# Attention ahead of two expert layers: exponentials behind all maxima of their banks, new engine orders, diagonal forms of q copied by GpSimd

## The chip, the core and the metric

The program runs on one core of a Trainium2 chip. Its time is the device time of one execution in microseconds. TensorE (PE) multiplies, VectorE (DVE), ScalarE (ACT) and GpSimd (POOL) work beside it, and SyncE (SP) issues most transfers. Each engine takes its instructions in the order in which the program gives them.

## The reference

Inputs are in float32. First comes attention over 2 batches, 8 heads, 576 rows and 64 columns a head, with a mask by blocks of 64 rows; then two layers of experts on the 1152 rows of 512 columns.

```python
scores = (1 / np.sqrt(D)) * np.matmul(q, k.transpose(0, 1, 3, 2))
scores = np.where(block_i >= block_j, scores, -1e9)
attn = np.exp(scores - np.max(scores, axis=-1, keepdims=True))
attn = attn / (np.sum(attn, axis=-1, keepdims=True) + 1e-09)
x = np.matmul(attn, v)            # heads side by side: rows of 512 columns
# layer 1: the best of 8 experts for each row, relu(x @ w1[e]) @ w2[e], times two gates
# layer 2: the same with one gate, and at most `capacity` rows an expert, in order of the rows
```

## The kernel before, in words

**Precision.** A matmul operand is held as two halves, a high one (`kh`, `nh`, `wh`, `xh`: a copy rounded by ACT) and a low one (`kl`, `nl`, `wl`, `xl`: the rest, by VectorE), and three products replace one.

**Packs and stages.** A head's nine blocks of rows, of both batches, are split into three packs (L96). Pack 0 has four units: block pairs of 384 columns at columns 0 (unit 0) and 512 (unit 1), and of 128 columns at 896 (unit 2) and 384 (unit 3). Pack 1 has two units of 512 columns. Pack 2 has three single blocks: 576 columns at 256 (unit 0), 256 at 0 (unit 1), 192 at 832 (unit 2). A unit's scores lie in a tile `s` of two PSUM banks of 512 columns each, of which there are two. A stage is one pack of one head, 24 in all: heads 0 to 4 one after the other with packs 0, 1, 2 each, and then heads 5, 6, 7 with pack 0 of all three, pack 1 of all three, pack 2 of all three.

**A stage's work.** TensorE makes the scores; VectorE takes the maximum of each unit (`greatest`, tile `mx`, "m0" to "m3"); ACT takes the exponential with that maximum and sums it (`power`, tile `p`, "e0" to "e3"); TensorE turns the results in groups (`transp`, into a bank `pst`); ACT copies the first group out and VectorE the others (`turned`, tile `tp`, "tp0" to "tp2"); TensorE multiplies by v (`pv`, into the one bank `po`); ACT copies that out (`put_out`, tile `ot` or `of`); TensorE multiplies by an identity beside gate columns (`with_gates`, "mv", into the same bank); and VectorE divides by the sums (`inverse`, "ri") and stores rows and gate logits (`results`, "x", tiles `x` and `lg`). GpSimd adds the logits over heads, except for the last head.

**q and k of a head.** TensorE turns them ("K", "Q" for the first 512 rows and "R" for the last 64), ACT makes high halves and VectorE low halves. Pack 2's single blocks need q in diagonal form (`qh`, `ql`: each batch's 64 columns in their own quarter, the rest zero). For blocks 2 and 3 this is "B", read from Q's bank; for block 8 it is part of "R".

**The order.** For stage i the loop of L1803 puts into TensorE's queue: R's turns, the scores of stage i+1, mv of i-2, the turned groups of i, K and Q of a later head, pv of i-1. ACT's and VectorE's queues follow the lists `ORDER` by the pack of stage i; their m and e are those of stage i+1, ri, x and ot those of i-2, tp that of i. `weave` (L1742) then takes, in rounds, the head of each queue whose named predecessors are done, and issues it. That order is the program; the class `InOrder` (L32) keeps it on each engine. Waits between engines follow from it: an instruction waits for earlier accesses of the same tile by another engine. Other instructions, of GpSimd and the routing's small steps, are placed by a planner.

**Into the first expert layer.** When head 7's pack 0 is stored, a routing of the first 384 rows begins (`begin_first`): three products ("route1" to "route3") with small VectorE steps between, the load of the chosen expert's weights, and the gathers of three items' rows by GpSimd. The weights' splits W0 to W3 (`split_hi`, L196) are tied to instructions of the last stage (L1874), the low ones (`split_lo`, L214) to the routing's results. Behind the last mv, `xprep` (L811) turns the first item's rows, and `begin_known` (L982) starts its products and the routing of all rows (L593).

Of the kernel before, what the change touches and what calls it, by code (L numbers as in the profile page):

```python
# [50 lines left out]
def kernel(  # L51
# [1312 lines left out]
    with ExitStack() as actx:  # L1364
# [127 lines left out]
        def q_high(h):  # L1492
            s = st[h]
            for n in ("nh", "nl"):
                s[n] = ap3.tile([P, NC4 * P], F32R, tag=n, name=f"{n}{h}")
            AS.activation(s["nh"], s["ps"]["q"], AF.Copy, scale=SCALE)

        def q_low(h):
            s = st[h]
            AV.scalar_tensor_tensor(out=s["nl"], in0=s["ps"]["q"], scalar=SCALE, in1=s["nh"].bitcast(F32), op0=ALU.mult, op1=ALU.subtract)  # L1500

        def blocks(ps):
            return [ps[r, :].rearrange("p (b j) -> p b j", j=BLK) for r in halves]

        def b_high(h, ps, b0, b1):
            for r, x in zip(halves, blocks(ps)):
                AS.activation(st[h]["qh"][r, b0:b1, r], x, AF.Copy, scale=SCALE)

        def b_low(h, ps, b0, b1):
            for r, x in zip(halves, blocks(ps)):  # L1510
                AV.scalar_tensor_tensor(out=st[h]["ql"][r, b0:b1, r], in0=x, scalar=SCALE, in1=st[h]["qh"][r, b0:b1, r].bitcast(F32), op0=ALU.mult, op1=ALU.subtract)
# [199 lines left out]
        def route_steps(n):  # L1711
            for _ in range(n):
# [15 lines left out]
            ),  # L1728
# [26 lines left out]
        def bank(*names):  # L1755
# [8 lines left out]
            "B": (("S", lambda h: b_high(h, st[h]["ps"]["q"][:, 2 * BLK : 4 * BLK], 0, 2)), ("V", lambda h: b_low(h, st[h]["ps"]["q"][:, 2 * BLK : 4 * BLK], 0, 2))),  # L1764
# [3 lines left out]
        def turn_op(h, nm):  # L1768
            lows = (("V", nm, h), ("V", "B", h)) if nm == "Q" else (("V", nm, h),)
            put("P", ("P", nm, h), bank(*lows), turn, h, nm.lower())  # L1770

        def split_op(eng, nm, h):
            dep = ("S", nm, h) if eng == "V" else ("P", "Q" if nm == "B" else nm, h)
            put(eng, (eng, nm, h), (dep,), dict(split_ops[nm])[eng], h)

        def units(i):
            return [(("S", "e", i, u), ("V", "m", i, u)) for u in range(len(packs[stages[i][1]]))]

        def score_op(i):
# [17 lines left out]
        waiting["B"] = 0  # L1797
        score_op(0)
        for u, (e, m) in enumerate(units(0)):
            put("V", m, [("P", "S", 0)], greatest, *stages[0], u)  # L1800
            put("S", e, [m], power, *stages[0], u)
        n = len(stages)
        for i in range(n + 2):  # L1803
# [11 lines left out]
            if i == known_at + 5:  # L1815
                put("P", ("P", "route3"), bank(), route_steps, 3)
            if i + 1 < n:
                score_op(i + 1)
                h1, p1 = stages[i + 1]
                for u, (e, m) in enumerate(units(i + 1)):  # L1820
                    toks["V", f"m{u}"] = lambda m=m, u=u: put("V", m, [("P", "S", i + 1)], greatest, h1, p1, u)
                    toks["S", f"e{u}"] = lambda e=e, m=m, u=u: put("S", e, [m], power, h1, p1, u)
            if 0 <= i - 2 < n:
# [5 lines left out]
                toks["V", "ri"] = lambda: put("V", ("V", "ri", i - 2), [e for e, _ in units(i - 2)], inverse, h2, p2)  # L1829
# [9 lines left out]
            if i < n:  # L1839
                h, _ = stages[i]  # L1840
                for g in range(len(groups[pk])):
                    t = (COPY[pk, g], "tp", i, g)
                    put("P", ("P", "T", i, g), list(bank(t)) + [e for e, _ in units(i)], transp, h, pk, g)
# [3 lines left out]
            for h_, at_ in turns.items():  # L1847
                if at_ == i:
# [3 lines left out]
                    waiting["B"] = h_  # L1852
            if 0 <= i - 1 < n:
                h0, p0 = stages[i - 1]
                deps = [(COPY[p0, g], "tp", i - 1, g) for g in range(len(groups[p0]))]
                if i >= 2:
# [7 lines left out]
            for eng in "SV":  # L1864
                for t in ORDER[eng][pk].split():
# [7 lines left out]
        item0["w1"] = []  # L1873
# [241 lines left out]
```

## Time and profile before

| | us |
|---|---|
| median of 3 runs | 426.58 (423.88 to 428.85) |
| profiled execution | 430.7 |
| its span, first to last instruction | 429.0 |
| busy: TensorE, VectorE, ACT, GpSimd | 377.0, 292.8, 243.4, 103.8 |

The mean granted clock of TensorE is 0.964 of 2.4 GHz. Attention lies in the first 160 us of the span, the first expert layer from there to about 300 us, and the second behind it. A busy time says how long an engine had an instruction at work; what an engine waited for stands in square brackets behind the first instruction after the wait.

### The profile page before, as it was taken

The page shows a single profiled execution, that of the slowest core. Times are in us where ns is not written, and L with a number is a line of the kernel's source. Part 1 is how long each engine was busy: PE and PEld are TensorE (multiplying, and loading weights), DVE is VectorE, ACT ScalarE, POOL GpSimd, SP SyncE. Part 2 cuts the span into 40 slices and gives each one's busy share as a digit, 9 for nine tenths or more (in the row PEclk, how much of TensorE's full clock was granted, in tenths as well). Part 3 has the DMA queues.
Part 4 walks back from the last instruction along what each step waited for, and adds up shares of the span by engine and source line. Part 5 has one row for each costly group of instructions (what it writes and reads, how often), then busy time and mean ns, then how long its engine had stood idle before and what let it go on. Part 6 is the DMA issues. An engine that isn't in the chain of part 4 may idle for free.

```text
span 429.0 us, 7864 instructions
## 1 busy us (share of the span) xinstructions
PE 377.0 (88%) x2501; PEld 296.6 (69%) x2501; DVE 292.8 (68%) x733; ACT 243.4 (57%) x487; POOL 103.8 (24%) x240
## 2 busy tenths in 40 slices
PE   5777877867677679999999999999999899999993
PEld 4667766756666567888888888477577687885551
DVE  2565656766647856959988995747979899991110
ACT  2565646555644544347878782245377699892110
POOL 8110610000100430322213310176132017720010
PEclk9998969998989977999999999999999999999998
DMA  6653299030102750059629209789689589999970
GB/s 136 119 114 79 57 324 282 8 84 2 29 24 76 281 178 21 9 191 297 242 83 338 95 26 323 259 330 291 208 271 350 205 308 354 402 333 365 395 242 24
DMA packets 65238, 83.14 MB, mean 194 GB/s; under 512 B 34432, under 2 KB 39040, under 8 KB 65188
## 3 DMA queue, kind: packets, MB, share of 16 engines
q1 hardware_dynamic: 62212, 72.98, 51.4%
q0 software_dynamic: 2976, 9.58, 6.2%
q8 instruction: 22, 0.36, 0.3%
q14 instruction: 28, 0.23, 0.2%
HBM read 91.83 MB, written 11.80 MB: 242 GB/s over the span
## 4 chain that ended last, share of the span: by engine, by line
PE 56%; DVE 17%; DMA 10%; ACT 7%; issue 7%; SPq 1%; POOLq 0%; DVEq 0%; ACTq 0%
PE py L842 12%; DMA raw<-in_moe_w_dram 10%; PE ph L828 9%; PE po L40 7%; PE s L40 5%; ACT p L40 5%; PE ph L1220 4%; PE pst L40 4%; DVE mx L40 4%; PE ph L1195 3%; DVE wl L214 3%; PE ph L884 2%; DVE wl_a L214 2%; DVE wl_b L214 2%; PE py L956 1%
## 5 line engine op out<-in xcount | busy, mean ns | idle before, releaser
L40 ACT ACTIVATE p<-s,mx 128x384 f32<-128x384 f32 (+5 forms) x72 | 39.3, 546 | 44.9 <-DVE mx L40 43.4
L214 DVE TENSOR_TENSOR wl<-raw,wh 128x1024 fp32r<-128x1024 f32 x52 | 61.6, 1222 | 2.3 <-ACT wh L196 2.2
L40 DVE TENSOR_REDUCE mx<-s 128x1 f32<-128x384 f32 (+5 forms) x72 | 36.6, 509 | 34.0 <-ACT p L40 23.4
L196 ACT CAST wh<-raw 128x1024 fp32r<-128x1024 f32 x52 | 51.5, 1063 | 2.3 <-DMA raw<-in_moe_w_dram 1.6
L40 PE MATMUL po<-tp,vn 128*64 128x128 f32 (+3 forms) x384 | 29.7, 301 | 18.5 <-issue 8.9
L828 PE MATMUL ph<-wh,xh 128*128 128x512 f32 x104 | 42.9, 413 | 0.0
L828 PE MATMUL ph<-wl,xh 128*128 128x512 f32 x104 | 41.1, 395 | 1.0 <-DVE wl L214 1.0
L828 PE MATMUL ph<-wh,xl 128*128 128x512 f32 x104 | 40.9, 393 | 0.0
L40 PEld LDWEIGHTS po<-tp,vn 128*64 128x64 f32 x384 | 23.3, 147 | 24.9 <-issue 17.3
L214 DVE TENSOR_TENSOR wl_a<-raw,wh_a 128x1024 fp32r<-128x1024 f32 x28 | 33.2, 1217 | 2.0 <-ACT wh_a L196 1.8
L196 ACT CAST wh_a<-raw 128x1024 fp32r<-128x1024 f32 x28 | 28.1, 1067 | 6.0 <-DMA raw<-in_moe_w_dram 6.0
L40 PE MATMUL pst<-ident,p 128*128 128x128 f32 x200 | 29.1, 291 | 2.5 <-ACT p L40 2.2
L214 DVE TENSOR_TENSOR wl_b<-raw,wh_b 128x1024 fp32r<-128x1024 f32 x24 | 28.4, 1217 | 0.0
L40 PEld LDWEIGHTS pst<-ident,p 128*128 128x128 f32 x200 | 25.1, 152 | 3.8 <-ACT p L40 2.7
L847 POOL DMA_INDIRECT out_dram<-ys,ig x7 | 10.2, 1455 | 66.3 <-ACT ys L1042 51.0
L842 PE MATMUL py<-wh_a,hh 128*128 128x512 f32 x64 | 26.1, 409 | 0.0
L842 PE MATMUL py<-wh_a,hl 128*128 128x512 f32 x64 | 25.1, 392 | 0.1
L842 PE MATMUL py<-wl_a,hh 128*128 128x512 f32 x64 | 25.1, 392 | 0.0
L196 ACT CAST wh_b<-raw 128x1024 fp32r<-128x1024 f32 x24 | 23.8, 1066 | 0.8 <-DMA raw<-in_moe_w_dram 0.8
L828 PEld LDWEIGHTS ph<-wl,xh 128*128 128x128 f32 x104 | 19.6, 188 | 5.5 <-DVE wl L214 2.3
L828 PEld LDWEIGHTS ph<-wh,xl 128*128 128x128 f32 x104 | 19.5, 188 | 4.6 <-DVE xl L818 0.4
L828 PEld LDWEIGHTS ph<-wh,xh 128*128 128x128 f32 x104 | 19.6, 188 | 4.2 <-ACT hs L886 0.4
(452 smaller groups left out, 895.4 us busy)
## 6 DMA issues: line engine op xcount, KB each, us to landing
raw<-in_moe_w_dram SPq DMA_DIRECT2D x124, 512.0 KB
rx<-in_moe_w_dram SPq DMA_DIRECT2D x28, 512.0 KB
out_dram<-zrow SPq DMA_DIRECT2D x9, 256.0 KB
x2d<-zrow SPq DMA_DIRECT2D x9, 256.0 KB
kn<-in_k_dram SPq DMA_DIRECT2D x16, 128.0 KB
qn<-in_q_dram SPq DMA_DIRECT2D x16, 128.0 KB
vn<-in_v_dram SPq DMA_DIRECT2D x16, 128.0 KB
x1d<-x SPq DMA_DIRECT2D x2, 576.0 KB
```

What stands on the lines that cost most here:

```text
L40: r = f(*args, **kw)
L196: nc.scalar.copy(whs[i], raw[:, c, :] if src is None else src)
L214: V.tensor_tensor(wls[i], raw[:, c, :] if src is None else src, whs[i].bitcast(F32), op=ALU.subtract)
L828: yield nc.tensor.matmul(out_, l[:, c * P : (c + 1) * P], r[:, cols], start=(c == 0 and j == 0), stop=(c == KD - 1 and j == 2))
L842: nc.tensor.matmul(y, l[:, cs], r[:, rs], start=(first and j == 0), stop=(last and j == 2))
L847: nc.gpsimd.indirect_dma_start(out=dest, out_offset=bass.IndirectOffsetOnAxis(ap=io.bitcast(U32), axis=0), in_=ys, in_offset=None, bounds_ ...
L884: nc.tensor.matmul(ps, l[:, c * P : (c + 1) * P], r[:, i * 512 : (i + 1) * 512], start=(n == 0), stop=(n == 3 * KD - 1))
L956: nc.tensor.matmul(y, l[:, (f % 4) * P : (f % 4 + 1) * P], r[:, (f % 2) * 512 : (f % 2 + 1) * 512], start=(j == f == 0), stop=(j == 2 and ...
L1195: nc.tensor.matmul(hp[r, :], xt[:, c * P + k * BLK : c * P + (k + 1) * BLK], w[c][:, z * 512 : (z + 1) * 512], start=(c == 0), stop=(c == ...
L1220: nc.tensor.matmul(y[d][r, 0:256], ht[:, j * P + z * BLK : j * P + (z + 1) * BLK], w[f // 2][:, (f % 2) * 512 + d * 256 : (f % 2) * 512 + ...
```

## The change

- `power` is now issued behind the maxima of all units that share a bank with its own, not behind its own alone.
- `ORDER` has other lists. K and Q go ahead of ot where the next maxima are of pack 2, and behind it elsewhere; there tp0 goes ahead of the exponentials, whose order is 1, 2, 0. Where the next maxima are of pack 0, maxima 0 and 3 (bank 0) come first, then x, 1 and 2; exponentials come as 0, 3, 1, 2.
- The split instructions of q's diagonal forms go: the R piece of q joins `nh` and `nl`, which have 576 columns now, and GpSimd copies 12 blocks of 64x64 a head from them into `qh` and `ql`.
- The last three rounds have lists of their own (`LAST`): W0 to W3, three low splits L0 to L2, and the first item's rows (X: turned on TensorE ahead of the last two mv and the last pv) are in the queues. The last pv has a bank of its own, so that it does not wait for x.

```diff
-            AS.activation(s["nh"], s["ps"]["q"], AF.Copy, scale=SCALE)
+            AS.activation(s["nh"][:, c], s["ps"][nm][:, 0 : c.stop - c.start], AF.Copy, scale=SCALE)
...
+        def diagonal(h, b0):
+            s = st[h]
+            for b, j in SOLO.items():
+                if (j < 2) == (b0 == 0):
+                    for x, y in (("qh", "nh"), ("ql", "nl")):
+                        for r in halves:
+                            nc.gpsimd.tensor_copy(s[x][r, j, r], s[y][r, b * BLK : (b + 1) * BLK].bitcast(F32))
...
         def r_low(h):
             s = st[h]
-            ps = s["ps"]["r"]
-            b_low(h, ps[:, 0:BLK], 2, 3)
-            c = slice(NC4 * P, S)
-            AV.tensor_tensor(s["kl"][:, c], ps[:, BLK : 2 * BLK], s["kh"][:, c].bitcast(F32), op=ALU.subtract)
+            q_low(h, RC, "r")
+            AV.tensor_tensor(s["kl"][:, RC], s["ps"]["r"][:, BLK : 2 * BLK], s["kh"][:, RC].bitcast(F32), op=ALU.subtract)
+            diagonal(h, 0)
+            diagonal(h, 2)
...
-            po = s["po"][pk] = ps_t.tile([P, 512], F32, tag="po", name="po", bufs=1)
+            po = s["po"][pk] = pst() if (h, pk) == stages[-1] else ps_t.tile([P, 512], F32, tag="po", name="po", bufs=1)
...
         ORDER = {
             "S": (
-                "K Q B ot0 ot1 ot2 R tp0 e0 e1 tp1 e2 e3",
-                "ot0 ot1 ot2 K Q B R e0 tp0 e1 tp1 e2 e3",
-                "K Q B ot0 ot1 ot2 R e0 tp0 e1 tp1 e2 e3",
+                "ot0 ot1 ot2 K Q R tp0 e0 e3 e1 e2 tp1",
+                "K Q ot0 ot1 ot2 R tp0 e1 e2 e0 e3 tp1",
+                "ot0 K Q ot1 ot2 R e0 tp0 e3 e1 tp1 e2",
             ),
             "V": (
-                "K Q B ri m0 R m1 x m2 tp0 m3 tp1 tp2",
-                "K ri R m0 m1 x Q B m2 tp0 m3 tp1 tp2",
-                "K Q B ri R m0 x m1 m2 m3 tp0 tp1 tp2",
+                "K Q ri m0 m3 R m1 x m2 tp0 tp1 tp2",
+                "K ri R m0 m1 x m2 m3 Q tp0 tp1 tp2",
+                "K Q ri R m0 m3 x m1 m2 tp0 tp1 tp2",
             ),
         }
+        LAST = {
+            "S": ("ot0 ot1 ot2 W0 tp0 W1", "ot0 ot1 ot2 X W2", "ot0 ot1 ot2 W3"),
+            "V": ("ri x tp1 tp2 L0", "ri x X L1", "ri x L2"),
+        }
+        def x_turn():
+            item0["ps"] = pst()
+            for c in range(KD):
+                PE.transpose(item0["ps"][:, c * P : (c + 1) * P], item0["xg"][0][:, c * P : (c + 1) * P], ident)
...
         def units(i):
-            return [(("S", "e", i, u), ("V", "m", i, u)) for u in range(len(packs[stages[i][1]]))]
+            us = packs[stages[i][1]]
+            banks = [set(range(o // 512, (o + n - 1) // 512 + 1)) for _, _, o, n in us]
+            return [(("S", "e", i, u), ("V", "m", i, u), [("V", "m", i, w) for w in range(len(us)) if banks[w] & banks[u]]) for u in range(len(us))]
...
+            if i == n:
+                put("P", ("P", "X"), list(bank(("V", "X"))) + [("P", "route3")], x_turn)
...
-                    toks["S", f"e{u}"] = lambda e=e, m=m, u=u: put("S", e, [m], power, h1, p1, u)
+                    toks["S", f"e{u}"] = lambda e=e, ms=ms, u=u: put("S", e, ms, power, h1, p1, u)
...
-        for c, w in enumerate(("p", "p", "tp", "ot")):
-            with tc.issue_after(anchors[w, H - 1, 2]):
-                item0["w1"].append(split_hi(c))
-            if c < KD - 1:
-                with tc.issue_after(first1["found" if c else "placed"]):
-                    split_lo(c)
...
-        item0["xs"], item0["low"] = xprep(item0["xg"][0], PX.next(), True, True)
-    with tc.issue_after(last[0]):
-        one.begin_known(item0["xs"], item0["low"], item0["w1"], item0["xg"])
+        one.begin_known(item0["xs"], lambda: None, item0["w1"], item0["xg"])
```

## Rows read from the trace of the kernel before

**Rows 1.** The page's part 1: busy us, share, instructions of each engine.

```profile
PE 377.0 (88%) x2501; PEld 296.6 (69%) x2501; DVE 292.8 (68%) x733; ACT 243.4 (57%) x487; POOL 103.8 (24%) x240
```

**Rows 2.** Busy by stretch: length, PE, PEld, DVE, ACT, POOL, PEclk, DMA.

```profile
67.00:85.00 18.00, 13.87 (x137) 11.96 (x137) 11.74 (x35) 10.92 (x36) 1.81 (x8) 1.00 0.41 116
...
39.90:43.30 3.40, 3.40 (x23) 3.30 (x20) 1.84 (x6) 1.45 (x5) 0.19 (x1) 0.50 0.00 0
...
57.00:63.80 6.80, 6.80 (x44) 6.04 (x42) 3.53 (x11) 2.87 (x10) 0.51 (x2) 0.50 1.03 346
...
118.60:120.75 2.15, 0.01 (x2) 0.04 (x2) 1.26 (x4) 1.39 (x4) 0.03 (x1) 1.00 0.00 0
...
156.00:166.20 10.20, 8.82 (x39) 7.09 (x40) 4.17 (x15) 2.53 (x7) 0.28 (x1) 0.50 0.08 22
170.00:340.00 170.00, 169.30 (x989) 130.24 (x988) 135.85 (x326) 101.45 (x140) 45.10 (x56) 1.00 0.64 221
```

**Rows 3.** TensorE's timeline, 67 to 86 us: start, length, instruction, [idle before].

```profile
68.88 1.22 PE L40 MATMUL po<-tp,vn 128*64 128x192 f32 x20 [0.78 <-DVE lg L40]
...
71.59 0.64 PE L40 MATMUL po<-mv,ot 128*128 128x160 f32 x4
...
75.36 1.09 PE L40 MATMUL po<-tp,vn 128*64 128x256 f32 x12 [2.26 <-issue]
...
85.50 0.71 PE L40 MATMUL po<-tp,vn 128*64 128x192 f32 x6 [0.50 <-DVE lg L40]
```

**Rows 4.** ACT's timeline, 67 to 86 us.

```profile
69.15 0.19 ACT L40 ACTIVATION_READ_ACCUMULATOR p<-s,mx 128x1 f32 x1
70.15 0.59 ACT L40 COPY ot<-po 128x128 f32<-128x128 f32 x3 [0.80 <-PE po L40]
70.76 0.59 ACT L40 CAST kh<-pst 128x512 fp32r<-128x512 f32 x1
```

**Rows 5.** VectorE's timeline, 67 to 86 us.

```profile
67.84 0.69 DVE L40 TENSOR_REDUCE mx<-s 128x1 f32<-128x512 f32 x1 [0.90 <-ACT p L40]
...
71.38 0.69 DVE L40 TENSOR_TENSOR kl<-pst,kh 128x512 fp32r<-128x512 f32 x1 [1.95 <-ACT kh L40]
...
72.64 0.73 DVE L40 TENSOR_REDUCE mx<-s 128x1 f32<-128x576 f32 x1
74.33 0.42 DVE L40 TENSOR_REDUCE mx<-s 128x1 f32<-128x256 f32 x1 [0.96 <-ACT p L40]
...
84.46 0.69 DVE L40 TENSOR_REDUCE mx<-s 128x1 f32<-128x512 f32 x1 [0.62 <-ACT p L40]
```

**Rows 6.** VectorE's timeline, 84 to 131 us: a second maximum.

```profile
113.01 0.55 DVE L40 TENSOR_REDUCE mx<-s 128x1 f32<-128x384 f32 x1
```

**Rows 7.** Timeline, 48 to 67 us: pack 1's second maximum.

```profile
48.86 0.69 DVE L40 TENSOR_REDUCE mx<-s 128x1 f32<-128x512 f32 x1 [0.40 <-ACT p L40]
```

**Rows 8.** GpSimd's copies of line 1425: ns min/median/max.

```profile
L1425 POOL COPY mv<-ident x15: 228/234/241, 5.0 to 8.0; 64x64 f32<-64x64 f32 x15
```

**Rows 9.** GpSimd by line, 140 to 160 us: busy us, mean ns.

```profile
L537 POOL TENSOR_SCALAR a_ne<-a_eo,a_ef 128x8 f32<-128x8 f32 x1 | 1.4, 1401 | 0.1
```

**Rows 10.** TensorE's timeline, 84 to 132 us.

```profile
91.45 0.66 PE L40 MATMUL pst<-ident,kn 128*128 128x128 f32 x4 [1.72 <-ACT tp L40]
...
101.78 1.12 PE L40 MATMUL pst<-ident,qn 128*128 128x128 f32 x4 [2.01 <-DVE tp L40]
...
131.27 1.09 PE L40 MATMUL po<-tp,vn 128*64 128x128 f32 x16 [1.32 <-DVE lg L40]
```

**Rows 11.** ACT's timeline, 128 to 172 us.

```profile
143.83 1.05 ACT L196 CAST wh<-raw 128x1024 fp32r<-128x1024 f32 x1 [1.64 <-DMA raw<-in_moe_w_dram]
```

**Rows 12.** TensorE's timeline, 130 to 172 us.

```profile
150.42 0.72 PE L40 MATMUL po<-mv,ot 128*128 128x160 f32 x4 [1.80 <-ACT ot L40]
...
167.06 0.20 PE L593 MATMUL pz<-ohx,ltri 128*128 128x80 bf16 x1
```

**Rows 13.** The gathered rows' tile, 120 to 172 us: its transfers.

```profile
DMA to landing us min/median/max: 5.0/8.0/8.1
```

More of the change, by code (lines that the diff above doesn't have):

```diff
@@ L1502, in blocks @@
[L1502 to L1511, printed above, removed]
+            if nm == "q":
+                for n in ("nh", "nl"):
+                    s[n] = ap3.tile([P, S], F32R, tag=n, name=f"{n}{h}")
@@ new lines, in q_high, with q_low @@
+            AS.activation(s["nh"][:, c], s["ps"][nm][:, 0 : c.stop - c.start], AF.Copy, scale=SCALE)
+        def q_low(h, c=QC, nm="q"):
+            s = st[h]
+            AV.scalar_tensor_tensor(out=s["nl"][:, c], in0=s["ps"][nm][:, 0 : c.stop - c.start], scalar=SCALE, in1=s["nh"][:, c].bitcast(F32), op0=ALU.mult, op1=ALU.subtract)
+        def diagonal(h, b0):
[5 more added lines that the diff above has]
+                            nc.gpsimd.tensor_copy(s[x][r, j, r], s[y][r, b * BLK : (b + 1) * BLK].bitcast(F32))
@@ L1724, with w_high, w_low, x_high @@
             "S": (
[3 rows of a table removed]
[3 rows of a table added]
             ),
             "V": (
[3 rows of a table removed]
-            ),
-        }
[3 rows of a table added]
+            ),
+        }
+        LAST = {
+            "S": ("ot0 ot1 ot2 W0 tp0 W1", "ot0 ot1 ot2 X W2", "ot0 ot1 ot2 W3"),
+            "V": ("ri x tp1 tp2 L0", "ri x X L1", "ri x L2"),
+        }
+        def w_high(c):
+            item0["w1"].append((whs[c], wls[c]))
+            AS.copy(whs[c], raw[:, c, :])
+        def w_low(c):
+            AV.tensor_tensor(wls[c], raw[:, c, :], whs[c].bitcast(F32), op=ALU.subtract)
+        def x_turn():
+            item0["ps"] = pst()
+            for c in range(KD):
+                PE.transpose(item0["ps"][:, c * P : (c + 1) * P], item0["xg"][0][:, c * P : (c + 1) * P], ident)
+        def x_high():
+            item0["xs"] = XH.next(), XL.next()
+            for c in (slice(0, DM // 2), slice(DM // 2, DM)):
+                AS.copy(item0["xs"][0][:, c], item0["ps"][:, c])
+        def x_low():
+            xh, xl = item0["xs"]
+            AV.tensor_tensor(xl, item0["ps"], xh.bitcast(F32), op=ALU.subtract)
+        item0["w1"] = []
         queues = {"P": [], "S": [], "V": []}
@@ L1796 @@
             split_op("V", nm, 0)
-        waiting["B"] = 0
         score_op(0)
-        for u, (e, m) in enumerate(units(0)):
+        for u, (e, m, ms) in sorted(enumerate(units(0)), key=lambda x: x[0] in (1, 2)):
             put("V", m, [("P", "S", 0)], greatest, *stages[0], u)
-            put("S", e, [m], power, *stages[0], u)
+        for u, (e, m, ms) in sorted(enumerate(units(0)), key=lambda x: x[0] in (1, 2)):
+            put("S", e, ms, power, *stages[0], u)
         n = len(stages)
@@ L1828 @@
                     toks["S", f"ot{j}"] = lambda x=x, j=j: put("S", x, [("P", "pv", i - 2)], put_out, h2, p2, j)
-                toks["V", "ri"] = lambda: put("V", ("V", "ri", i - 2), [e for e, _ in units(i - 2)], inverse, h2, p2)
+                toks["V", "ri"] = lambda: put("V", ("V", "ri", i - 2), [e for e, _, _ in units(i - 2)], inverse, h2, p2)
                 def both(h, pk):
@@ L1842 @@
                     t = (COPY[pk, g], "tp", i, g)
-                    put("P", ("P", "T", i, g), list(bank(t)) + [e for e, _ in units(i)], transp, h, pk, g)
+                    put("P", ("P", "T", i, g), list(bank(t)) + [e for e, _, _ in units(i)], transp, h, pk, g)
                     k = len(tps) - 6
@@ L1851 @@
                         waiting[nm] = h_
-                    waiting["B"] = h_
             if 0 <= i - 1 < n:
@@ L1855 @@
                 deps = [(COPY[p0, g], "tp", i - 1, g) for g in range(len(groups[p0]))]
-                if i >= 2:
+                if i == n:
+                    deps += bank(("V", "x", n - 1))
+                elif i >= 2:
                     deps.append(("V", "x", i - 2))
@@ L1864 @@
             for eng in "SV":
-                for t in ORDER[eng][pk].split():
+                for t in (LAST[eng][i - n + 1] if i >= n - 1 else ORDER[eng][pk]).split():
                     f = toks.pop((eng, t), None)
```

32 lines of the change are left out of this document (16 added, 16 removed).

## Prediction

> **What bounds the kernel now.** The busy times come first: TensorE is busy 377.0 of 429.0 us [rows 1], and the table by stretch shows where it is not. From 170 to 340 us it is busy 169.3 of 170, while a full-clock stretch of attention, 67 to 85, has it busy 13.87 of 18 beside 11.74 on VectorE and 10.92 on ACT [rows 2]. No engine is full there: attention is a chain of waits. As TensorE is the bound once the experts run, what attention loses or gains moves the end one for one.
>
> The timelines of the three engines from 67 to 86 us then give the chain. A head is three stages (A, B, C: packs 0, 1, 2 being turned while the maxima are of pack 1, 2 and 0 of the next head), and one cycle runs from the product at 68.88 to that at 85.50, 16.6 us [rows 3]. The longest hole is in B: TensorE idles 2.26 us before the product at 75.36 [rows 3]. That product waits for the last reader of its bank, VectorE's x and lg. These stand behind the second maximum at 74.33, which idled 0.96 us until ACT's exponential was done; its first maximum, 72.64, came late because kl (71.38) waited for kh (70.76), and kh stood behind ot (70.15) on ACT [rows 4, 5].
>
> A maximum waits for every exponential of its stage that the program issues ahead of it, whatever the bank: at 84.46 the 512 columns of the second bank wait 0.62 us for the exponential of the first [rows 5]. The case where the program had two maxima ahead of the first exponential, 113.01, shows no such wait [rows 6]. So I read the change by which maxima its order issues first.
>
> The granted clock is the second loss: five stretches at 0.50, the 1.2 GHz level, the first at 39.9, the last up to 166.2 [rows 2]. One of them begins 1 us after the hole from 118.6 to 120.75, in which TensorE did 0.01 us of work [rows 2]. The cycle from 48.86 to 67.84, which holds the 6.8 us stretch, took 18.98 us against 16.62 for the next: 2.4 more [rows 2, 5, 7].
>
> **The change, part by part.** *Stage B.* ACT is free at 69.35, behind the readout of 69.15 [rows 4]. With K ahead of ot, kh starts there, not at 70.76; kl follows 0.62 behind and ends at 70.7; the reciprocals between it and the first maximum take 0.6 (72.64 less kl's end) and end at 71.3. The scores end at 71.6, where TensorE's next product starts [rows 3]. The first maximum then runs 71.7 to 72.4 and the second, with no wait, to 72.8; x and lg took the 0.6 up to 75.36, so the product starts at 73.4: **2.0 less**. ot, now behind K and Q, ends near 71.0, still before the scores. The scores of pack 0 keep their distance: what they need of Q on VectorE (a third maximum, under the second's 0.42, and nl, a shape like kl's 0.69) is done 1.0 behind x, about as long as the product lasts. The exponentials now wait for two or all three maxima; the copy tp0 is put ahead of them, so that TensorE's product does not wait for it.
>
> *Stage C.* By the order of the queues, maxima 0 and 3 come first, then exponential 0; maximum 1 is issued behind it and maximum 2 behind exponential 3, so two waits stay. Where two exponentials of a bank follow each other directly, one exchange of the engines is saved; I give it 0.2, bounds 0 and the 0.96 of one such wait [rows 5].
>
> *Stage A.* Pack 1's units have a bank each, so exponential 0 still goes ahead of maximum 1 and the wait of 84.46 stays. With its other durations as before, the product of 85.50 starts at 83.3, and one cycle is 14.4 us for 16.6: **2.2 us a head**, 6.6 for the three cycles that end at 84.46. Head 0 and the prologue have parts of it: bounds 0.3 (the prologue's maxima alone) and 3; I take 1.
>
> *Diagonal forms.* The split instructions of q's diagonals leave ACT and VectorE (three fewer on each per head; the R pieces are joined); that is in the cycle above. GpSimd gets 12 copies of 64x64 a head. The same shape took 0.234 us [rows 8]: 2.8 us a head, 22 us in all, on an engine busy 103.8 us [rows 1]. Only four of the 12 need R; all must be done before the scores of pack 2. Before, R's low half ends 0.62 ahead of 84.46, and the scores start when the product of 85.50 has run its 1.2 us: 2.9 us later [rows 3, 5]. By hand it comes 3.2 sooner, as the maxima ahead of it end sooner and the diagonals' low halves are gone, and the scores 2.2: 3.9 us of cover, enough even if all 12 follow R. No DMA is issued anew or moved past another. Their bound above is the slowest small GpSimd instruction, 1.40 us [rows 9], which ran beside VectorE's wl. I take 0.234, the row of the same shape, and keep the other for a rival. Lg additions and gate columns queue behind the copies on GpSimd; nothing near reads them. The Trainium skill (SBUF — State Buffer, who interferes with whom) says that a VectorE instruction with two SBUF inputs locks out a GpSimd instruction that reads SBUF. The 1.40 us agrees with it. By that rule the copies are safe here, since VectorE's long instructions inside a head read PSUM.
>
> *The late nine stages*, 84.5 to 150.4. Carrying the same steps on: the holes before 91.45 (1.72, behind tp0 and the exponential ahead of it), 101.78 (2.01, behind the alternating maxima and exponentials of pack 0), 120.75 (2.15) and 131.27 (1.32) go [rows 2, 10], together 7.2. Where packs 1 and 2 are in B and C the maxima are issued ahead of all exponentials. The first expert's weight split W0 now comes behind the last exponentials; before, ACT stood 1.64 us at 143.83 for the weights' transfer with an exponential behind it [rows 11]. Late, K and Q of head 7 now lie behind ot, where a hole of some 2.5 us stays. By hand the product after the last T comes 10 us sooner, 2 of it clock. A chain of nine stages by hand loses something at each wait: I take 7, bounds 3 and 10.
>
> *The last steps*, 150.42 to the routing's first product at 167.06, 16.6 us [rows 12]. The last product gets a bank of its own and no longer waits for x; the first item's rows are turned before it; W0 to W3 and L0 to L2 are placed between the copies. By hand 11.7 us remain: product at +4.2, its gates at +6.1, first expert products at +6.7, last split at +10.3. That is 4.9 less, part of which is the 10.2 us at 0.50 [rows 2]; I take 3.5, bounds 0 and 5. The moved transposes have a price: everything on TensorE now queues behind the gather, which lands 8.0 us after its issue [rows 13]. By hand it lands within 0.2 us of the time TensorE gets there; if the stages before shrink more, the gather is the next wait, up to 1 us.
>
> *Clock.* With the 2.2 us holes gone, the two stretches inside the cycles (2.4, and 1.2 for the one half as long) should mostly go. I take 1.5 of 3.6, as nothing shows how many a usual run has. Nothing behind 170 us changes but its start; the second expert layer's waits for weights hang on routing results that come as much sooner.
>
> Sum: 1 + 6.6 + 7 + 3.5 + 1.5 = **19.6 us**; with each term at its upper bound 28. The profiled execution took 430.7 us (span 429.0 and 1.7 around it), 4.1 above the median of 426.58. Off it the sum gives 411, off the median 407: **409 us**.
>
> **The rivals.** *Copies on the path (slower).* If GpSimd's copies are slowed like that of [rows 9], pack 2's scores wait for them. They begin to cost at 0.32 us a copy (3.9 over 12); from 0.5 on the cycle's 2.2 are gone too. At 0.8, midway between the two rows, five heads wait 5.7 us each, 28.5 less 19.6: **436 us**. For it: the 1.40 us; against it: 15 copies at 0.228 to 0.241 [rows 8]. Chance 0.07.
>
> *Waits taken over.* The exponentials now wait for the slowest maximum of their bank, ACT starts them later, and the copies stand behind them; only the 2.0 us of stage B remain, in four heads, 8 off the median: 419 us. For it: ACT already idles for maxima in every stage, and two of the waits stay in C. Chance 0.17.
>
> *By bank.* If maxima wait only for exponentials of their own bank, as the change's sets of banks assume, the waits left in A and C go too (0.62 and up to 0.96): 1.5 us a head more, 402 us. The Trainium skill (PSUM — Partial Sum Buffer, bank collisions) keeps engines apart by bank only. Here 84.46 is against it. Chance 0.06.
>
> *No effect.* That the new dependencies leave the issue order as it was, and the orders cancel: 426 us. The queue order speaks against it. Chance 0.05.
>
> **How the numbers follow.** The forecast has 0.65. Its low end is the median less 28, near 399; its high end meets the rival at 419. With 398 to 421 the rivals at 402 and 419 are inside and about 0.2 is left out. Beyond 1% (4.3 us; what a measurement of this kernel can tell from no change): faster 0.83, same 0.09, slower 0.08.
>
> **What would show it.** After: kh before ot in stage B; no second maximum of pack 2 waiting for ACT; TensorE's 2.2 us hole in B gone and a head's cycle near 14.4 us; the waits of pack 1's second maximum still there; 96 GpSimd copies near 0.23 us; the routing's first product near 147 us; fewer stretches at 0.50. The prediction is wrong if the cycle is above 16 us, if scores of pack 2 wait for GpSimd, if the turned rows wait for the gather by more than 2 us, or if stretches behind 170 us grow.

## The result, and the profile after

The kernel after takes **406.36 us**, median of four runs (405.0 to 410.33), beside 427.72 for the kernel before on the same chip: ratio 0.953, 95% interval 0.944 to 0.962. I had said 409. The profiled execution of after took 406.61 us (span 404.9), that of before 430.7 (span 429.0): 24.1 us of span to account for.

The busy times of after, to stand beside [rows 1]: GpSimd has 96 instructions and 21.6 us more, ACT and VectorE 24 instructions less each.

```profile
PE 368.0 (91%) x2501; PEld 289.5 (72%) x2501; DVE 285.4 (70%) x709; ACT 233.6 (58%) x463; POOL 125.4 (31%) x336
```

VectorE's timeline of after from 55 to 75 us, for [rows 5] (start, length, instruction, [idle before and what ended it]):

```profile
58.64 0.69 DVE L40 TENSOR_REDUCE mx<-s 128x1 f32<-128x512 f32 x1 [1.53 <-ACT p L40]
...
62.59 1.09 DVE L40 TENSOR_REDUCE mx<-s 128x1 f32<-128x576 f32 x2 [0.57 <-PE s L40]
...
68.18 0.56 DVE L40 TENSOR_REDUCE mx<-s 128x1 f32<-128x384 f32 x1 [0.20 <-ACT p L40]
69.27 0.29 DVE L40 TENSOR_REDUCE mx<-s 128x1 f32<-128x128 f32 x1 [0.53 <-ACT p L40]
...
73.14 0.69 DVE L40 TENSOR_REDUCE mx<-s 128x1 f32<-128x512 f32 x1 [1.52 <-ACT p L40]
```

Pack 2's two large maxima now run back to back at 62.59 and wait for TensorE alone; the 0.96 us of 74.33 [rows 5] is gone. Pack 1's second maximum still idles 1.5 us for an exponential, in the other bank. From 58.64 to 73.14 a head takes 14.50 us; before it took 16.62 [rows 5].

ACT and TensorE of after in the same stretch, for [rows 4] and [rows 3]:

```profile
60.05 0.58 ACT L40 CAST kh<-pst 128x512 fp32r<-128x512 f32 x1
...
61.00 0.58 ACT L40 COPY ot<-po 128x128 f32<-128x128 f32 x3
```

```profile
64.27 1.09 PE L40 MATMUL po<-tp,vn 128*64 128x256 f32 x12 [0.36 <-PE pst L40]
...
78.64 0.66 PE L40 MATMUL pst<-ident,kn 128*128 128x128 f32 x4 [0.24 <-ACT tp L40]
...
85.63 0.66 PE L40 MATMUL pst<-ident,kn 128*128 128x128 f32 x4 [1.44 <-ACT tp L40]
...
87.27 1.11 PE L40 MATMUL pst<-ident,qn 128*128 128x128 f32 x4 [0.98 <-DVE tp L40]
...
95.48 1.22 PE L40 MATMUL po<-tp,vn 128*64 128x192 f32 x20 [2.36 <-DVE lg L40]
...
104.44 1.09 PE L40 MATMUL po<-tp,vn 128*64 128x256 f32 x12 [0.28 <-PE pst L40]
...
112.30 1.09 PE L40 MATMUL po<-tp,vn 128*64 128x128 f32 x16 [0.33 <-DVE lg L40]
...
131.58 0.72 PE L40 MATMUL po<-mv,ot 128*128 128x160 f32 x4 [1.70 <-ACT ot L40]
...
134.37 0.66 PE L40 MATMUL pst<-ident,xg 128*128 128x128 f32 x4
...
142.44 0.50 PE L884 MATMUL ph<-wl,xh 128*128 128x512 f32 x1 [2.54 <-DVE wl L40]
...
144.36 0.20 PE L593 MATMUL px<-ohx,ltri 128*128 128x80 bf16 x1
```

kh stands ahead of ot, and the hole of 2.26 us before stage B's product has become 0.36. Of the late holes of before, those ahead of 91.45, 101.78, 120.75 and 131.27 [rows 2, 10] are ahead of 78.64, 87.27, 104.44 and 112.30 now: 1.72, 2.01, 2.15 and 1.32 us have become 0.24, 0.98, 0.28 and 0.33. The turning of head 7's K (85.63) still waits 1.44 us for tp0, and the hole at 95.48 is left. The gathered rows are turned at 134.37 without a wait. From the product at 131.58 to the routing's first at 144.36 are 12.78 us, 16.64 before [rows 12], 2.54 of them one wait.

Half clock is down from five stretches [rows 2] to two, in the table by stretch of after (PEclk is the third number from the end):

```profile
87.18:90.59 3.41, 3.32 (x24) 2.66 (x25) 0.37 (x2) 0.75 (x6) 0.00 (x0) 0.50 0.00 0
124.73:128.14 3.41, 3.41 (x18) 3.37 (x17) 2.01 (x9) 0.00 (x0) 2.74 (x3) 0.50 0.84 311
```

Where the 24.1 us of span came from, by the starts of the same instructions in both traces:
- up to pack 1's second maximum of head 1 (31.02 before, 29.59 after): 1.4
- the three cycles to head 4's (84.46 and 73.14): 9.9. At full clock a cycle gained 2.12, or 6.4 in three; the other 3.5 are the two half-clock stretches that lay inside
- the late nine stages, to the product with gates (150.42 and 131.58): 7.5, with 6.8 us at half clock in both
- the last steps, to the routing's first product: 3.9
- behind it: 1.4 (261.9 and 260.5)

### The profile page after: what moved, and what is told of

It reads as the page before. It is cut to its first block, busy times and chain, and to the rows that moved or that the text cites. A ratio compares the mean times of both kernels' runs of the same rounds, so it can differ in the third digit from the quotient of the medians.

```text
span 404.9 us, 7910 instructions
## 1 busy us (share of the span) xinstructions
PE 368.0 (91%) x2501; PEld 289.5 (72%) x2501; DVE 285.4 (70%) x709; ACT 233.6 (58%) x463; POOL 125.4 (31%) x336
## 4 chain that ended last, share of the span: by engine, by line
PE 41%; DMA 10%; DVE 9%; issue 3%; ACT 1%; SPq 1%; POOLq 0%; DVEq 0%
PE py L842 12%; DMA raw<-in_moe_w_dram 10%; PE ph L828 10%; PE ph L1220 4%; PE ph L1195 3%; DVE wl_a L214 2%; DVE wl L214 2%; PE ph L884 2%; PE py L956 1%; DVE wl_b L214 1%; PE pz L1963 1%; PE px L2011 1%; PE pz L2011 1%; PE px L814 1%; PE px L1963 1%
## 5 line engine op out<-in xcount | busy, mean ns | idle before, releaser
L214 DVE TENSOR_TENSOR wl<-raw,wh 128x1024 fp32r<-128x1024 f32 x49 | 58.0, 1221 | 2.5 <-ACT wh L196 2.2
L40 ACT ACTIVATE p<-s,mx 128x128 f32<-128x128 f32 (+5 forms) x72 | 38.9, 545 | 28.7 <-DVE mx L40 27.5
L40 DVE TENSOR_REDUCE mx<-s 128x1 f32<-128x128 f32 (+5 forms) x72 | 34.9, 507 | 26.9 <-PE s L40 13.7
L196 ACT CAST wh<-raw 128x1024 fp32r<-128x1024 f32 x48 | 47.3, 1063 | 1.3 <-DMA raw<-in_moe_w_dram 1.3
L40 PE MATMUL po<-tp,vn 128*64 128x128 f32 (+3 forms) x364 | 26.9, 291 | 9.6 <-DVE lg L40 6.9
L40 PEld LDWEIGHTS po<-tp,vn 128*64 128x64 f32 x364 | 20.9, 140 | 15.5 <-PE pst L40 5.7
L40 PE MATMUL pst<-ident,p 128*128 128x128 f32 x200 | 28.2, 284 | 1.2 <-ACT p L40 1.1
L40 PEld LDWEIGHTS pst<-ident,p 128*128 128x128 f32 x200 | 24.0, 147 | 2.5 <-ACT p L40 2.2
L40 ACT COPY tp<-pst 128x512 f32<-128x512 f32 (+1 forms) x24 | 13.1, 548 | 21.8 <-PE pst L40 21.7
L847 POOL DMA_INDIRECT x2d<-ys,io x6 | 7.5, 1253 | 50.5 <-ACT ys L1042 42.6
L828 PEld LDWEIGHTS ph<-wl,xh 128*128 128x128 f32 x104 | 19.6, 189 | 4.8 <-DVE wl L214 1.5
```

What stands on the lines that cost most here:

```text
L40: r = f(*args, **kw)
L196: nc.scalar.copy(whs[i], raw[:, c, :] if src is None else src)
L214: V.tensor_tensor(wls[i], raw[:, c, :] if src is None else src, whs[i].bitcast(F32), op=ALU.subtract)
L828: yield nc.tensor.matmul(out_, l[:, c * P : (c + 1) * P], r[:, cols], start=(c == 0 and j == 0), stop=(c == KD - 1 and j == 2))
L847: nc.gpsimd.indirect_dma_start(out=dest, out_offset=bass.IndirectOffsetOnAxis(ap=io.bitcast(U32), axis=0), in_=ys, in_offset=None, bounds_ ...
```

## The experiments

All runs in one table. Cycle: from head 3's second maximum of pack 1 to head 4's. Late: from there to the last exponential's readout. Last: from that readout to the routing's first product. Half clock: time at 1.2 GHz between 10 and 172 us, and in brackets how much of it lies in the late stretch. Ratios are to the kernel before in the same set of runs.

| kernel | median us | ratio (95%) | cycle | late | last | half clock |
|---|---|---|---|---|---|---|
| before | 427.72 | 1 | 16.6 | 65.2 | 17.4 | 27.3 (6.8) |
| after | 406.36 | 0.953 (0.944 to 0.962) | 14.5 | 57.7 | 13.5 | 6.8 (6.8) |
| own_max | 413.66 | 0.973 (0.964 to 0.982) | 14.75 | 58.2 | 15.1 | 13.7 (6.8) |
| old_orders | 413.40 | 0.971 (0.964 to 0.978) | 16.0 | 57.9 | 14.0 | 6.8 (3.4) |
| old_both | 420.85 | 0.979 (0.969 to 0.988) | 16.7 | 59.8 | 14.8 | 13.7 (0) |
| splits_back | 413.92 | 0.966 (0.958 to 0.974) | 14.5 | 63.4 | 13.5 | 13.7 (13.7) |
| old_last | 413.12 | 0.973 (0.964 to 0.982) | 14.5 | 59.4 | 16.1 | 10.2 (6.8) |
| copies_x3 | 425.80 | 0.997 (0.992 to 1.002) | 14.5 | 56.8 | 14.0 | 20.5 (6.8) |
| copies_x3_late | 419.02 | 0.986 (0.981 to 0.991) | 14.5 | 59.7 | 14.9 | 23.9 (13.7) |
| maxima_apart | 408.81 | 0.952 (0.946 to 0.958) | 14.5 | 57.9 | 13.5 | 10.2 (6.8) |
| pack1_too | 405.31 | 0.941 (0.933 to 0.949) | 13.4 | 60.0 | 14.9 | 17.1 (13.7) |
| wl_first | 406.53 | 0.950 (0.943 to 0.957) | 14.5 | 57.5 | 12.5 | 10.2 (6.8) |
| after_again | 407.97 | 0.951 (0.944 to 0.958) | 14.5 | 57.7 | 13.5 | 6.8 (6.8) |
| three_edits | 401.29 | 0.939 (0.934 to 0.944) | 13.4 | 56.2 | 12.5 | 6.8 (6.8) |

Medians of single kernels scatter by some microseconds with the half-clock stretches, so the parts are read from the three columns of the trace, and the ratio says only whether the kernel got slower. The columns are of one execution each, and a stretch at half clock lengthens the column in which it lies. In the late column this can be priced: copies_x3 and copies_x3_late have the same program there and took 56.8 us with 6.8 at half clock and 59.7 with 13.7; pack1_too, with 13.7, took 2.3 more than after. By estimate, then, 6.8 us more at half clock cost 2 to 3 us in the late column. Three rows of the table by stretch, for after, old_both and splits_back, show how far apart the clocks were (0.94, 1.00 and 0.89):

```profile
73.14:130.85 57.71, 46.47 (x442) 39.77 (x442) 41.02 (x159) 29.96 (x100) 18.01 (x69) 0.94 0.30 92
```

```profile
82.72:142.53 59.81, 43.60 (x444) 37.15 (x442) 40.45 (x154) 31.74 (x100) 16.08 (x59) 1.00 0.25 77
```

```profile
73.08:136.47 63.39, 49.92 (x443) 42.34 (x442) 43.72 (x168) 32.46 (x108) 9.84 (x33) 0.89 0.28 85
```

**own_max**: the exponentials wait for their own maximum alone.

```diff
-put("S", e, ms, power, h1, p1, u)
+put("S", e, [m], power, h1, p1, u)
```

> The kernel after, except that each exponential again waits for its own maximum alone; orders, GpSimd copies and last steps stay as changed. If the issue order decides (a maximum waits for every exponential of its stage that is issued ahead of it), the exponentials slip back between the maxima: in stage B the second maximum of pack 2 waits about 1 us for ACT again, in stage C the second maximum of bank 0 as well, 1.5 to 2 us a head and as much in the late stages, 8 to 14 us in all: 414 to 420 us against 406.4. If only the place of K, Q and ot mattered, at most 2 us: 406 to 408.

Measured 413.66, and the span 3.3 above after's. The number of the first theory was nearly met, its reason was not: the cycle grew by 0.25 only. The new orders alone keep pack 2's maxima together (63.60 x2 in the first row below); the waits come back in stage C, 1.54 us for 0.73, and most of that is made up for by a shorter wait of pack 1's second maximum (0.96 us at 74.38, for 1.52). Of the 3.3 us, the three cycles give 1.2, the late stages 0.5 and the last steps 1.6; 3.4 us of these lie at half clock, and none in after. VectorE of own_max:

```profile
63.60 1.09 DVE L40 TENSOR_REDUCE mx<-s 128x1 f32<-128x576 f32 x2 [0.58 <-PE s L40]
...
68.96 0.29 DVE L40 TENSOR_REDUCE mx<-s 128x1 f32<-128x128 f32 x1 [0.80 <-ACT p L40]
...
71.07 0.29 DVE L40 TENSOR_REDUCE mx<-s 128x1 f32<-128x128 f32 x1 [0.74 <-ACT p L40]
```

**old_orders**: the order lists of before, without their B.

```diff
-"K Q ot0 ot1 ot2 R tp0 e1 e2 e0 e3 tp1",
+"ot0 ot1 ot2 K Q R e0 tp0 e1 tp1 e2 e3",
...
-"K ri R m0 m1 x m2 m3 Q tp0 tp1 tp2",
+"K ri R m0 m1 x Q m2 tp0 m3 tp1 tp2",
```

> The kernel after with the two order lists of the kernel before (their B tokens gone), the new dependencies, GpSimd copies and last steps kept. If the order is the main cause, TensorE's hole of 2 us in stage B is back (kh behind ot on ACT), with some half-clock stretches: 5 heads by 2 us and 2 to 4 of clock, 416 to 420 us. If the dependencies do most of it, the waits of maxima stay gone and the time stays within 3 us of 406.4.

Measured 413.40, between my two ranges; the cycle is 1.5 us longer, and the hole before stage B's product is back with 1.20 us. ACT and TensorE of old_orders:

```profile
64.23 0.59 ACT L40 COPY ot<-po 128x128 f32<-128x128 f32 x3 [0.55 <-PE po L40]
64.84 0.59 ACT L40 CAST kh<-pst 128x512 fp32r<-128x512 f32 x1
```

```profile
68.39 0.87 PE L40 MATMUL po<-tp,vn 128*64 128x256 f32 x8 [1.20 <-issue]
```

So the order is worth 1.5 us a head. In the late stages the column is that of after (57.9 us), but with 3.4 us at half clock in place of 6.8; at the same clock it would be 1 to 1.5 us longer by the estimate above. The half-clock stretches of the cycles did not come back with the orders.

**old_both**: both of these at once.

> The kernel after with both the old order lists and the old dependencies (each exponential waits for its own maximum); GpSimd copies and last steps kept. Singly, either cost some 3 to 6 us of the profiled span. If they are two halves of one mechanism (either keeps the maxima ahead of the exponentials in the late stages), both together bring the late stages back to 62 to 65 us and the time to 418 to 422. If they are independent and the late gain lies with the diagonals or the last steps, the late stages stay near 58 us and the time is 413 to 416.

Measured 420.85. The cycle is 16.7, that of before: with diagonals on GpSimd but old orders and dependencies no head is shorter. Either half brings part of the 2.1 us (0.7 the dependencies, 1.9 the orders), not the sum. The late stages grew by 2.1 us, but none of them lay at half clock, where after had 6.8 us: at after's clock they would be 4 to 5 us longer by the estimate above, which is my first reading. The waits say the same. The hole in stage B is back, and so are the late holes of before, 2.01, 2.16 and 1.32 us where after had 0.98, 0.28 and 0.33. TensorE of old_both:

```profile
73.60 1.09 PE L40 MATMUL po<-tp,vn 128*64 128x256 f32 x12 [2.27 <-issue]
...
98.14 0.66 PE L40 MATMUL pst<-ident,qn 128*128 128x128 f32 x4 [2.01 <-DVE tp L40]
...
115.45 1.09 PE L40 MATMUL po<-tp,vn 128*64 128x256 f32 x12 [2.16 <-issue]
...
125.29 1.09 PE L40 MATMUL po<-tp,vn 128*64 128x128 f32 x16 [1.32 <-DVE lg L40]
```

**splits_back**: q's diagonal forms on ACT and VectorE again.

```diff
-nc.gpsimd.tensor_copy(s[x][r, j, r], s[y][r, b * BLK : (b + 1) * BLK].bitcast(F32))
+AS.activation(st[h]["qh"][r, b0:b1, r], x, AF.Copy, scale=SCALE)
+AV.scalar_tensor_tensor(out=st[h]["ql"][r, b0:b1, r], in0=x, ...)
```

> The kernel after with q's diagonal forms split on ACT and VectorE again, as before (three instructions on each per head), and no copies on GpSimd; dependencies, orders and last steps as changed. The late nine stages (last pack 1 maximum of head 4 to the last exponential) took 65.2 us before and 57.7 after, and 57.9 with the old orders, so orders alone did not shorten them. If the move of the diagonals did, they are back near 62 to 64 us and the cycle of a head (14.5 us) grows by 0.5 to 1: 412 to 417 us. If, as my prediction had it, the diagonals' move is small and the late stages gained from the maxima that go first, 406 to 409.

Measured 413.92. The cycle is unchanged: the low halves fall into the time in which pack 1's second maximum waits anyway (1.08 us of wait in place of 1.52). The late stages are 5.7 us longer, between 82 and 107 us, where K and Q of heads 6 and 7 are turned: the turned bank is free only when VectorE's ql has read it, and the half-clock stretches there grow from 3.4 to 10.2 us. By the estimate above, 2 to 3 of the 5.7 us go with the clock (13.7 us of the late stages at half clock, for 6.8), and 3 to 4 are left for the diagonals. VectorE, then TensorE of splits_back:

```profile
73.08 0.69 DVE L40 TENSOR_REDUCE mx<-s 128x1 f32<-128x512 f32 x1 [1.08 <-ACT p L40]
```

```profile
80.04 0.66 PE L40 MATMUL pst<-ident,qn 128*128 128x128 f32 x4 [0.80 <-DVE ql L40]
...
94.94 0.63 PE L40 MATMUL pst<-ident,p 128*128 128x128 f32 x4 [0.69 <-DVE ql L40]
```

**old_last**: the last steps of before (weight splits anchored behind exponentials, rows turned behind the attention, the last product in the shared bank).

> The kernel after with the last steps of the kernel before: no list for them, the first expert's weight splits and the turning of the first rows back behind the attention, the last product back in the shared bank. If the last steps gave what the traces show (the distance from the last product with gates but two to the routing's first product fell from 16.6 to 12.8 us, and ACT no longer stood for weights ahead of an exponential, 1.6 us), 410 to 412 us. If that part was paid by the clock or is hidden behind the gather, 406 to 407.

Measured 413.12, a little above my range, and 4.2 us later at the routing's product. The weight split makes most of it, in two places. ACT's first one waits for its transfer; VectorE's low half waits for it, and the last stage's first maximum starts behind that, at 128.50 for 126.71 in after, and the exponentials with it. Then two more splits, 2.00 us, stand ahead of ot on ACT. ACT, VectorE and TensorE of old_last; after had 131.58 for the last:

```profile
126.20 1.05 ACT L196 CAST wh<-raw 128x1024 fp32r<-128x1024 f32 x1 [2.60 <-DMA raw<-in_moe_w_dram]
...
132.55 2.00 ACT L196 CAST wh<-raw 128x1024 fp32r<-128x1024 f32 x2
```

```profile
127.28 1.23 DVE L214 TENSOR_TENSOR wl<-raw,wh 128x1024 fp32r<-128x1024 f32 x1 [1.96 <-ACT wh L196]
```

```profile
135.09 1.25 PE L40 MATMUL po<-mv,ot 128*128 128x160 f32 x4 [4.18 <-ACT ot L40]
```

**copies_x3**: every diagonal copy three times (`halves * 3`).

> The kernel after with each of GpSimd's 96 diagonal copies issued three times over, 0.78 us in place of 0.26. If the copies are off the path with 3.3 us to spare (in the trace after, the four that need R take 1.1 us, end at 57.56 and the scores that read them start at 60.83, and the other eight run a stage earlier), the time stays within 2 us of 406.4. If copies of this length are on the path as my rival had it (they begin to cost at 0.32 us, and at 0.8 five heads wait 5.7 us each), 430 to 436 us.

Measured 425.80: my forecast failed, and the rival's place failed too. TensorE waits for a diagonal copy twice and nowhere else. TensorE and, for the second wait, GpSimd of copies_x3:

```profile
26.01 0.58 PE L40 MATMUL s<-kh,qh 128*128 128x256 f32 x1 [9.30 <-POOL qh L1512]
...
62.53 0.58 PE L40 MATMUL s<-kh,qh 128*128 128x256 f32 x1 [5.90 <-POOL qh L1512]
```

```profile
50.59 0.20 POOL L114 MEMSET ones_bf<- 128x128 bf16 x1
...
56.50 0.18 POOL L1707 CAST capf<-capi 128x1 f32<-128x1 int32 x1
56.63 0.51 POOL L1512 CAST qh<-nh 64x64 fp32r<-64x64 f32 x2
...
60.78 1.69 POOL L1512 CAST qh<-nh 64x64 fp32r<-64x64 f32 x6
```

From 50.59 to 56.63 GpSimd runs the routing's constants; the copies of head 2 stand behind them in its queue, with some of head 3's among them, and the last of them ahead of the scores ends at 62.47. So the 5.90 us are the length of the copies, since in this head nothing covers it. In heads 1, 3 and 4 three times the copies cost nothing (cycle 14.5).

**copies_x3_late**: three times from head 2 on, once before it.

> The kernel after with GpSimd's diagonal copies issued three times over from head 2 on, once in heads 0 and 1. With all heads three times, 426 us, the trace shows TensorE waiting for a copy twice only: 9.30 us in head 0, where the copies stood around the copies of the gate columns that wait for their transfer, and 5.90 us in head 1, where they stood behind GpSimd's set-up work for the routing. If it is the queue in those two heads, the time is now 405 to 409 us, without a wait for GpSimd. If the length of the copies itself costs (contention with VectorE, or later heads), 412 us or more.

Measured 419.02, a miss of its first number, by my own slip: the second wait is at pack 2's scores of head 2, not of head 1, so this kernel kept it. It shows the place all the same. Head 0's 9.30 us are gone, head 2's wait is the one for GpSimd left, and head 4's cycle is 14.5:

```profile
52.42 0.58 PE L40 MATMUL s<-kh,qh 128*128 128x256 f32 x1 [5.92 <-POOL qh L1512]
```

The 11.3 us at the routing's product are this wait and 17 us more at half clock, of which 6.8 begin in it.

**maxima_apart**: a tile of its own for each unit's maxima.

```diff
-out=s["mx"][:, t : t + 1]
+out=s["mx"][t]
```

> The kernel after with a small tile of its own for each unit's maxima (11 of one column in place of one of 11 columns); nothing else. My theory so far, that a maximum waits for every exponential of its stage issued ahead of it because both read the scores: pack 1's second maximum still idles 1.5 us for ACT, 406 us. The rival: the wait hangs on the tile of the maxima, which the exponential reads and the next maximum writes: then no maximum waits for ACT any more (1.5 us at 73.14, 0.2 and 0.5 in stage C), pack 1's product starts 1.0 us sooner in each head, cycle near 13.3 us, 398 to 401 us.

Measured 408.81, cycle 14.5, and the wait stays. The tile of the maxima is not its cause.

```profile
74.46 0.69 DVE L40 TENSOR_REDUCE mx<-s 128x1 f32<-128x512 f32 x1 [1.52 <-ACT p L40]
```

**pack1_too**: pack 1's exponentials behind both maxima.

```diff
-if banks[w] & banks[u]]
+if len(us) == 2 or banks[w] & banks[u]]
```

> The kernel after, except that pack 1's exponentials too wait for both maxima of their stage, so that both maxima are issued ahead of the first exponential. If the order of issue makes the wait, the 1.5 us before pack 1's second maximum go, the product behind it starts 1.0 us sooner, the exponentials 0.6 later: cycle 13.5 for 14.5 us, 399 to 402 us. If the wait then only moves to the exponentials, whose rows TensorE turns next, 405 to 407.

The wait is gone and the cycles to heads 2 and 4 take 13.4 us, 1.1 less, as the first theory had it. VectorE of pack1_too:

```profile
69.19 0.68 DVE L40 TENSOR_REDUCE mx<-s 128x1 f32<-128x512 f32 x1
```

The time is 405.31 all the same: 4.0 us ahead of after at 69.19, it is 0.3 ahead at the routing's product, its profiled execution having 17.1 us at half clock for 6.8. (The four executions of this kernel had mean clocks from 0.970 to 0.987, the profiled one 0.975.) The cycle between them, to head 3, stayed at 14.5; 0.74 of the 1.1 us is a wait for head 2's copies, whose cover was used up. TensorE:

```profile
44.77 0.39 PE L40 MATMUL s<-kh,qh 128*128 128x256 f32 x1 [0.74 <-POOL qh L1512]
```

**wl_first**: on VectorE, the third weight chunk's low half ahead of the last x.

```diff
-"V": ("ri x tp1 tp2 L0", "ri x X L1", "ri x L2"),
+"V": ("ri x tp1 tp2 L0", "ri x X L1 L2", "ri x"),
```

> The kernel after with only the low half of the third weight chunk moved ahead of the last x on VectorE. If that half, queued behind another chunk's low half (138.79) and the last x, is why the last steps gave 3.9 us where my working by hand had 4.9, TensorE's wait of 2.54 us at 142.44 goes and the routing's first product comes 0.7 us sooner, 143.6 for 144.36, no more, as VectorE then bounds it: 405 to 407 us. If the wait only moves to the next low half, no change of the routing's product.

The wait of 2.54 us is gone and the routing's product comes 11.72 us behind the product with gates (132.33 to 144.05), 1.06 sooner than in after; VectorE bounds it now. The time, 406.53, can't tell this from no change. TensorE of wl_first:

```profile
132.33 0.72 PE L40 MATMUL po<-mv,ot 128*128 128x160 f32 x4 [1.45 <-ACT ot L40]
...
144.05 0.20 PE L593 MATMUL px<-ohx,ltri 128*128 128x80 bf16 x1 [1.61 <-DVE ohx L254]
```

**after_again**:

> The kernel after once more, unchanged, to stand beside the two others on the same chip. 405 to 410 us, as before.

Measured 407.97 (404.91 to 412.04). Behind the routing's product its trace took 263.4 us, after's 260.5.

**three_edits**: pack1_too, wl_first, and lists of their own for the two late stages in which pack 0 is turned and pack 0 is next.

```diff
+PK0 = {"S": "K Q ot0 ot1 ot2 R tp0 e0 e3 e1 e2 tp1", "V": "K Q ri m0 m3 x R m1 m2 tp0 tp1 tp2"}
```

> The kernel after with three edits against its remaining holes: pack 1's exponentials behind both maxima (as in the run before); the low half of the third weight chunk issued ahead of the last x, for TensorE's 2.54 us at 142.44; and, in the two late stages where pack 0 is turned while pack 0 is next, K and Q ahead of ot on ACT and x ahead of R and m1 on VectorE, for the 2.36 us at 95.48. If each hole was a wait that these orders make: 1 us (measured), 0.7 us (VectorE's routing step ends at 143.57 and bounds it) and 1.9 us, with the half-clock stretch that begins behind the late hole mostly gone: 400 to 403 us. If the waits only move, or the half-clock stretches come back elsewhere (the run with pack 1's edit had 0.975), 404 to 407.

Measured **401.29** (400.21 to 401.73), faster than after beside it (407.97, lowest 404.91) and the best of all. TensorE's hole of 95.48 is gone, half clock is 6.8 us, and the late stages lost 1.5 us, the last 1.0. Its six executions had mean clocks from 0.989 to 0.993. TensorE's first product of the routing, 144.36 in after:

```profile
137.59 0.20 PE L593 MATMUL px<-ohx,ltri 128*128 128x80 bf16 x1 [1.60 <-DVE ohx L254]
```

## Why the prediction was right, and where not

**Right in mechanism and size: the cycle.** 14.4 said, 14.50 found; kh ahead of ot, pack 2's maxima together, the hole in stage B 1.9 us shorter, two short waits left in stage C (0.20 and 0.53). One reading was off without a cost: the wait of pack 1's second maximum did not stay at 0.62 but grew to 1.52, as VectorE reaches it sooner; 0.44 of that is the diagonals' leaving (1.08 in splits_back). old_orders and old_both show that orders and dependencies carry it and the copies nothing. That a maximum waits for every exponential issued ahead of it, whatever the bank, held: the rival by bank fell with 1.52 us at 73.14, maxima_apart left the wait, and pack1_too removed it by order alone. Whether it hangs on the tile of the scores, which holds both banks, no run tried. The Trainium skill (PSUM — Partial Sum Buffer, bank collisions) asks for guards by bank and quadrant; this program waits for more, as the 1.52 us between two banks show.

**Right in size, with a part left out: the late nine stages.** 7 said, 7.5 found. I gave them to maxima issued ahead of exponentials and to the weight split, and the runs bear out both. Of the four holes that were to go, 7.2 us in before, 1.8 are left in after (0.24, 0.98, 0.28, 0.33), and old_both, without the new orders and dependencies, has 7.2 again (1.74 ahead of 89.72, and the three shown). At after's clock that is 4 to 5 us of the late column, by estimate. The weight split's part is 1.7 us (old_last). What I left out is the diagonals' leaving VectorE, by estimate 3 to 4 us here: I had counted it only in the cycle, where splits_back shows it to be worth nothing. So "that is in the cycle above" failed. The three parts add up to more than 7.5, so they are in part the same waits.

**Mis-sized: the clock.** 1.5 of 3.6 said, 3.5 found in the cycles; both stretches went, and did so in the second trace of after too. Part of this is the execution that happened to be profiled: its mean clock, 0.964, lies below 31 of the 38 other executions of before, from 0.948 to 0.986. How much the clock gives between usual executions, whose medians are 21.4 us apart and not 24.1, is open. **Head 0** gave 1.4 for 1. The 1.4 behind the routing's product is no effect: the second trace of after is 2.9 the other way.

**The last steps.** 3.5 said, 3.9 found. The 11.7 us worked out by hand were right but for one place: a fourth chunk's low half (VectorE, line 214, at 138.79) went ahead of the third's. wl_first, with the third's first, has 11.72. The gather was no wait. Before had 10.2 us of these steps at half clock and after none; no run separates that share of the 3.9.

**The sum.** 19.6 us stand beside 24.1 between the two profiled executions: the difference is mostly the clock's 2.0 and the 1.4 behind the routing's product. That 409 lies within 3 us owes something to taking the sum off a value midway between the profiled execution and the median. *No effect* falls with the 14.5 us cycle. *Waits taken over* has the heads nearly right, stage B's 1.9 of their 2.1 us; it falls by the late stages and the last steps, which it left as they were.

**Right outcome, wrong working: GpSimd's copies.** Their length held, and so did the reading of the Trainium skill (SBUF — State Buffer, who interferes with whom): none of the 96 was slowed. The 1.40 us behind the rival's price did not come again: the same instruction (L537) took 0.32 or 0.33 us in the 13 other traces. In before a wl on VectorE began 0.08 us behind it; in old_both one began 0.10 behind it and did not slow it, so what made the 1.40 is open. The copies' line in after (ns min/median/max):

```profile
L1512 POOL CAST qh<-nh x48: 229/233/237, 10.0 to 102.9; 64x64 fp32r<-64x64 f32 x48
L1512 POOL CAST ql<-nl x48: 229/234/237, 10.6 to 103.5; 64x64 fp32r<-64x64 f32 x48
```

The 3.9 us of cover, from the end of R's low half to the scores, came out at 3.6 to 3.7 in heads 1 to 4. What was wrong is that GpSimd is free in it. In heads 3 and 4 it is: only four copies follow R, with 3.3 us to spare. In head 2 nothing is to spare: GpSimd ends the routing's constants, and the four copies run from 45.41 to 46.51 while the scores that read them start. GpSimd and TensorE of after:

```profile
45.41 0.52 POOL L1512 CAST qh<-nh 64x64 fp32r<-64x64 f32 x2
46.00 0.51 POOL L1512 CAST ql<-nl 64x64 fp32r<-64x64 f32 x2
```

```profile
46.28 0.39 PE L40 MATMUL s<-kh,qh 128*128 128x256 f32 x1
```

I had looked at what queues behind the copies and not at what they queue behind. With 0.70 us of copying for each piece (three times 0.233) the rival's own working gives 22 us (12 times 0.70 less 3.9, in five heads). 19.4 came, but in two heads, where other work stood ahead of the copies, and part of it by the clock. Its chance of 0.07 rested on a margin that one head did not have. "Nothing near reads them", said of the gate columns, failed in head 0, where their copies wait for a transfer: TensorE waited 0.63 us for one in own_max, 0.92 in wl_first and 1.27 in maxima_apart, and not at all in after.

What stays open: how much of the 5.7 us of splits_back is the wait for ql and how much half clock, beyond the estimate; no run held the clock fixed.

## What to carry to other kernels

Before work goes to an engine off the path, read that engine's whole queue around each reader, in every iteration: one head with set-up work ahead of the copies had no cover, where its neighbours had 3 us. In programs of hand-written issue order, look at which instruction is issued first: moving a maximum ahead of an exponential removed a wait that separate tiles for the maxima did not, and that the exponential's other bank did not prevent. Judge a small edit by distances in the trace, as a gain of 4 us can vanish behind a few more half-clock stretches (pack1_too), and remove the next holes with it (three_edits). Before two distances are compared, see how much of each lies at half clock: the 2.1 us of old_both's late stages look like little until their clock is read beside after's.

## What the runs showed of the hardware

One added wait cost more than itself: copies_x3 lost 19.4 us against after by two waits of 15.2 together, and copies_x3_late 12.7 by one of 5.92, with 20.5 and 23.9 us at half clock for 6.8. Removing waits can go with more half clock too: pack1_too, busier in its heads (TensorE 38.0 of the 41.2 us of three cycles, for 38.0 of 43.6 in after), had 17.1 us at half clock. But three_edits, with the same edit in the heads, had 6.8, so that the one caused the other isn't shown.
